# Sigmoid attention and an MLP on one core: the attention's matmuls put in order by four heads instead of by two

## The chip, the cores and the metric

The kernel runs on one NeuronCore of a Trainium2 chip. The metric is the device time of one execution in microseconds (us); lower is better. The kernel before takes 1061.03 us, the median of three timed runs (1060.72 to 1061.9).

## What is computed

```python
def _attn_ref(q, k, v) -> np.ndarray:          # (8 batches, 12 heads, 448, 64), float32
    S = q.shape[2]
    scale = 1.0 / np.sqrt(q.shape[-1])
    scores = scale * np.matmul(q, k.transpose(0, 1, 3, 2)) - np.log(S)
    attn = 1.0 / (1.0 + np.exp(-scores))
    return np.matmul(attn, v).astype(np.float32)

def _moe_ref(x, w_in, w_out) -> np.ndarray:    # x (3584, 768), w_in (768, 2048), w_out (2048, 768)
    h = x @ w_in
    g = h * (1.0 / (1.0 + np.exp(-1.702 * h)))
    return (g @ w_out).astype(np.float32)

# reference: x is the attention's output, (batch, position) by (head, 64); result = _moe_ref(x, w_in, w_out)
```

## The kernel before, in words

The program has two stages. In the first, attention runs for 48 pairs of heads (8 batches, 6 pairs each) while VectorE (DVE) and ScalarE (ACT) unpack the weights beside it. In the second, the MLP runs over seven blocks of 512 rows: one block directly (`first_block`, L794), the rest in two groups of three by a scheme with fewer products (`triple`). This change touches the first stage alone.

A pair n of heads brings q and k into `qkraw` (`load_pair`, L518); `split_pair` (L541) makes of it `qk`, a rounded part (a cast, ACT L442 or DVE L443) and the rest (DVE L448). The 448 positions are three chunks of 128 keys and 64 left over. TensorE (PE) then has four kinds of work:

- S, `scores` (L567, matmuls L577): per pair and chunk c six matmuls, 64 rows by 128 columns of the array, out of `qk`. Three chunks are one S of a pair, 18 matmuls.
- L, `scores_left` (L585, matmuls L593): the left-over keys of two pairs together, 64 rows by 64 columns, straight from `qkraw`; 4 matmuls that the trace shows as 8.
- V, `values` (L601, matmuls L608): the product of a chunk's sigmoids with v, 128 rows by 64 columns; 2 matmuls per chunk, shown as 4, so 12 for a pair.
- VL, `values_left` (L615, matmuls L621): the product of the left-over keys, 64 by 64, shown as 8.

Each of S's chunks and each L fills a tile `sc` of two PSUM banks and is read by one sigmoid on ACT (L563), which writes a tile `a` in SBUF. All V and VL of two pairs (four heads) add into one tile `av` of two banks; `to_x` (L638) copies it out on ACT (L645) or DVE (L646), and DMAs spill it to DRAM. The eight banks are four such places, `q0` to `q3`; `two_banks(place)` (L555) takes them in turn, so a tile must have been read before the fourth tile after it can be begun.

The order of the work is set before the program runs, by a planner (`Plan.run`): it knows tasks with estimated costs and dependencies, takes PE's units in the order of the list that `attention` returns, begins a unit when its tasks that are `alone` are ready, and gives ACT, DVE and the DMA queue (SP) the task with the earliest due time. What it writes is four fixed lists of instructions; on the chip each engine works through its own list in order and waits on semaphores. A task in `round_and_rest`, `to_x` and the like that may run on ACT or DVE is given to one of them by the planner.

In the list before, the units of two pairs (n even, then n odd) are: S of the even pair with V of the odd pair before it and that group's VL; L of both pairs; S of the odd pair with V of the even pair. V of a pair thus comes one unit after its S.

`BUFS` (L27) says how many buffers a tile has in turn: `qk` 2, `vraw` 3, `a` 7, `al` (the sigmoids of an L) 1, `x32` (the copy of `av`) 3.

Of the kernel before, what the change touches and what calls it, by code (L numbers as in the profile page):

```python
# [24 lines left out]
WARM = 26  # L25

BUFS = dict(  # L27
    qk=2, vraw=3, a=7, al=1, raw64=2, e=4, qkraw=5, x32=3,
    pair=2, wsplit=4, q0=1, q1=1, q2=1, q3=1, h0=1, h1=1,
)  # L30
SLOTS = dict(s=1536, g=2048, t=384)
# [48 lines left out]
class Plan:  # L80
# [15 lines left out]
    def task(self, engine, cost, emit, deps=(), uses=()):  # L96
        return self.either({engine: cost}, {engine: emit}, deps, uses)
# [227 lines left out]
def sigmoid_attention_mlp(ctx: ExitStack, tc: tile.TileContext, qk, v, w, out):  # L325
# [11 lines left out]
    NC = S // P  # L337
# [48 lines left out]
    plan = Plan()  # L386
# [166 lines left out]
    place_of = {}  # L553
# [13 lines left out]
    def scores(n, c, t_s, s, place):  # L567
        ps, a = two_banks(place), buffer("a")

        terms = ((0, 1), (1, 0), (0, 0)) if n else ((0, 0),)  # L570

        def emit():
            make(ps, ps.tag, [P, 2, 512], F32, f"sc{n}_{c}")
            src = [s.tile[:, 0], s.tile[:, 1]] if n else [s.tile]
            for i, (kk, qq) in enumerate(terms):
                for j, rows in enumerate(halves_of_rows):
                    nc.tensor.matmul(  # L577
                        ps.tile[:, j, :S], lhsT=src[kk][rows, S + c * P : S + (c + 1) * P], rhs=src[qq][rows, :S],
                        start=i == 0, stop=i == len(terms) - 1,
                    )  # L580

        t = task("PE", (0.7, 0.61, 0.61)[c] if n else 0.9, emit, t_s, [ps, s])
        return t, sigmoid(f"a{n}_{c}", a, ps, t), a

    def scores_left(n, sources, place):  # L585

        ps, a = two_banks(place), buffer("al")

        def emit():
            make(ps, ps.tag, [P, 2, 512], F32, f"sc{n}_{NC}")  # L590
            for cols, (_, src) in zip(halves_of_rows, sources):
                for j, rows in enumerate(halves_of_rows):
                    nc.tensor.matmul(  # L593
                        ps.tile[cols, j, :S], lhsT=src.tile[rows, S + NC * P :], rhs=src.tile[rows, :S],
                        start=True, stop=True, skip_group_check=True,
                    )

        t = task("PE", 0.8, emit, [t for ts, _ in sources for t in ts], [ps, *(b for _, b in sources)])
        return t, sigmoid(f"a{n}_{NC}", a, ps, t, "al"), a

    def values(n, c, t_a, a, t_v, vr, ps):  # L601

        def emit():
            if ps.tile is None:
                make(ps, ps.tag, [P, 2, 512], F32, f"av{n}")
            for j, cols in enumerate(halves_of_rows):
                at = ((n % 2 * 2 + j) * NC + c) * D
                nc.tensor.matmul(  # L608
                    ps.tile[cols, n % 2, :S], lhsT=vr.tile[:, at : at + D], rhs=a.tile[:, j],
                    start=c == 0, stop=False, skip_group_check=True,  # L610
                )

        return task("PE", (0.8, 0.75, 0.75)[c], emit, [t_a, t_v], [ps, a, vr])

    def values_left(t_a, a, t_v, vr, ps):  # L615

# [6 lines left out]
                        start=False, stop=True, skip_group_check=True,  # L623
                    )

        return task("PE", 0.95, emit, [t_a, t_v], [ps, a, vr])

    def places(b):

# [6 lines left out]
    copies = []  # L636
# [33 lines left out]
        ), x)  # L670


    firsts, urgent = [], []

    def attention():

        units, late, held_ = [], [], 0
        for n, (b, p) in enumerate(pairs):
            t_q, qkr, t_v, vr = load_pair(b, p)
            t_s, s = split_pair(b, p, t_q, qkr)
            firsts.append(t_s)
            left = scores_left(n, [first, (t_q, qkr)], held_ + 1) if n % 2 else None
            chunks = [scores(n, c, [t_s] if n else t_q[: c + 1], s, held_ + 1 + n % 2 + c) for c in range(NC)]
            run = [t for t, _, _ in chunks]  # L690
            if n % 2 == 0:
                first, chunks0, pair0 = (t_q, qkr), chunks, (b, p)
            else:

                units.append([left[0]])
                held_ += 1
                ps = two_banks(held_)
                both = [
                    [values(m, c, got[1], got[2], t_v, vr, ps) for c, got in enumerate(cs)]
                    for m, cs in ((n - 1, chunks0), (n, chunks))  # L700
                ]
                both[1].append(values_left(*left[1:], t_v, vr, ps))
                late.append(both[0])
                copied = len(copies)
                to_x(*pair0, both[1][-1], ps)
                urgent.append(copies[copied:])
            if n > 2 and n % 2:

                plan.early += [(t, run[0]) for t in urgent[n // 2 - 1]]

            with_v = late.pop(0) if late else []
            for t in run[2:] + with_v:
                t.alone = False
            units.append(run + with_v)
            if n % 2:
                late.append(both[1])
        units.append(late.pop())
        place_of["next"] = held_ + 1
        return units

    FULL, PIECE, XB, GB = slice(0, N2), NW_EL, NJ * T, 4 * T
# [563 lines left out]
```

## Time and profile before

| what | value |
|---|---|
| median of three timed runs | 1061.03 us |
| span of the profiled execution, first to last instruction | 1056.4 us |
| the median less the span | 4.6 us |
| PE matmul, busy | 1042.8 us, 99% of the span |
| DVE, ACT busy | 836.1 us (79%), 558.8 us (53%) |
| attention, from PE's first scores to the end of the last VL | 4.0 to 259.7 us |

The page gives the profiled execution no time of its own beside its span; the 4.6 us between the span and the median lie around it. Busy PE time comes from modelled ends of matmuls, so that places where one matmul waits for another inside PE count as busy too. How long a run of matmuls takes is therefore read from when the next run's work begins or ends: in the chain of waits, a piece reaches from the end of the piece before to its own end.

### The profile page before, as it was taken

How to read it: one execution, taken by the hardware profiler on the slowest of the kernel's cores; microseconds unless marked ns; L12 is line 12 of the kernel's file. 1: busy time of each engine (PE TensorE's matmuls, PEld its weight loads, DVE VectorE, ACT ScalarE, POOL GpSimd, SP SyncE). 2: the span in 40 equal slices, each digit the busy share in tenths (PEclk: the TensorE clock that was granted, in tenths of full speed). 3: DMA queues.
4: the chain of work that ended last, by engine and by line, in shares of the span. 5: the costliest groups of instructions: out<-in, count | busy, mean ns of one | idle time of the engine just before them, and what ended most of it. 6: DMA issues, size and time to landing. Idle time of an engine off the chain costs nothing.

```text
span 1056.4 us, 13606 instructions
## 1 busy us (share of the span) xinstructions
PE 1042.8 (99%) x5300; PEld 777.6 (74%) x5300; DVE 836.1 (79%) x734; ACT 558.8 (53%) x519; POOL 0.2 (0%) x4
## 2 busy tenths in 40 slices
PE   9999999999999999999999999999999999999997
PEld 5454545454788888888887788888888888788886
DVE  5978788772999856787998989999884596888684
ACT  7889888785664523434554444333443263434342
POOL 0000000000000000000000000000000000000000
PEclk9999999999999999999999999999999999999999
DMA  9999997883899997767656665959775545445765
GB/s 365 346 379 353 317 393 264 312 298 113 314 396 387 353 391 248 245 190 238 221 167 209 224 211 181 306 195 363 274 234 200 187 147 182 145 155 153 234 203 187
DMA packets 114704, 271.44 MB, mean 257 GB/s; under 512 B 10320, under 2 KB 80080, under 8 KB 112592
## 3 DMA queue, kind: packets, MB, share of 16 engines
q1 hardware_dynamic: 114640, 270.57, 73.6%
q8 instruction: 42, 0.69, 0.3%
q14 instruction: 22, 0.18, 0.0%
HBM read 185.60 MB, written 84.93 MB: 256 GB/s over the span
## 4 chain that ended last, share of the span: by engine, by line
PE 93%; DVE 2%; ACT 2%; DMA 1%; SPq 0%; issue 0%; ACTq 0%
PE p L782 57%; PE av L608 11%; PE sc L577 9%; PE h L782 6%; PE o_q L782 6%; PE av L621 2%; PE sc L593 2%; DMA c<-wc 1%; ACT a L563 1%; DVE gs L725 0%; ACT o L1138 0%; ACT xp L996 0%; DMA w<-c 0%; SPq L416 0%; DVE xp L1008 0%; DVE o L1139 0%
## 5 line engine op out<-in xcount | busy, mean ns | idle before, releaser
L782 PE MATMUL p<-gp,w 128*128 128x512 f32 x1440 | 329.1, 389 | 2.3 <-DVE gp L1008 0.9
L782 PE MATMUL p<-xp,w 128*128 128x512 f32 x1440 | 327.8, 389 | 1.0 <-DVE xp L1008 1.0
L782 PEld LDWEIGHTS p<-gp,w 128*128 128x128 f32 x1440 | 269.8, 188 | 60.4 <-DVE gp L1008 1.7
L782 PEld LDWEIGHTS p<-xp,w 128*128 128x128 f32 x1440 | 270.3, 188 | 57.4 <-DVE xp L1008 1.4
L563 ACT ACTIVATE a<-sc,bias 128x896 f32<-128x896 f32 x168 | 156.3, 1012 | 20.1 <-PE sc L577 12.0
L608 PE MATMUL av<-a,vraw 128*64 128x448 f32 x576 | 118.6, 547 | 0.0
L577 PEld LDWEIGHTS sc<-qk 64*128 64x128 f32 x846 | 75.9, 184 | 39.3 <-issue 17.1
L577 PE MATMUL sc<-qk 64*128 64x448 f32 x846 | 98.1, 373 | 1.5 <-DVE qk L448 1.5
L608 PEld LDWEIGHTS av<-a,vraw 128*64 128x64 f32 x576 | 37.1, 136 | 59.5 <-issue 59.0
L1008 DVE TENSOR_TENSOR gp<-h,gp 128x2048 fp32r<-128x2048 f32 x31 | 70.9, 2288 | 9.3 <-ACT gp L996 8.9
L1138 ACT COPY h<-p 128x2048 f32<-128x2048 f32 x18 | 33.7, 1874 | 82.5 <-PE p L782 53.1
L782 PE MATMUL o_q<-g,w 128*128 128x512 f32 x288 | 66.5, 389 | 1.2 <-ACT graw L838 1.2
L782 PE MATMUL h<-x,w 128*128 128x512 f32 x288 | 66.5, 389 | 1.0 <-ACT x L645 1.0
L996 ACT CAST gp<-h 128x2048 fp32r<-128x2048 f32 x23 | 44.0, 1912 | 44.0 <-PE p L782 36.7
L1172 DVE TENSOR_TENSOR h<-h,p 128x2048 f32<-128x2048 f32 x23 | 52.1, 2283 | 17.6 <-PE p L782 10.4
L782 PEld LDWEIGHTS h<-x,w 128*128 128x128 f32 x288 | 54.0, 188 | 13.0 <-ACT x L645 1.8
L782 PEld LDWEIGHTS o_q<-g,w 128*128 128x128 f32 x288 | 54.0, 188 | 12.8 <-ACT graw L838 1.6
L1138 ACT COPY o<-p 128x1536 f32<-128x1536 f32 x18 | 25.9, 1443 | 59.2 <-PE p L782 19.2
L448 DVE TENSOR_TENSOR qk<-qkraw,qk 128x896 fp32r<-128x896 f32 x47 | 51.2, 1090 | 6.5 <-ACT qk L442 5.7
L725 DVE TENSOR_TENSOR h<-h,h 128x2048 f32<-128x2048 f32 x24 | 54.7, 2284 | 0.1
L745 ACT CAST wc<-ws 128x384 fp32r<-128x384 f32 (+1 forms) x57 | 32.2, 580 | 41.0 <-DVE ws L725 26.0
L996 ACT CAST xp<-x 128x1536 fp32r<-128x1536 f32 x19 | 28.1, 1479 | 39.1 <-PE p L782 31.4
(108 smaller groups left out, 969.1 us busy)
## 6 DMA issues: line engine op xcount, KB each, us to landing
w<-c SPq DMA_DIRECT2D x140, 384.0 KB, 4.4
w<-c SPq DMA_DIRECT2D x52, 768.0 KB, 4.7
w<-w SPq DMA_DIRECT2D x16, 1536.0 KB, 10.5
c<-wc SPq DMA_DIRECT2D x56, 384.0 KB, 5.6
qkraw<-qk SPq DMA_DIRECT2D x47, 448.0 KB, 7.5
vraw<-v SPq DMA_DIRECT2D x24, 448.0 KB, 5.2
c<-wc SPq DMA_DIRECT2D x14, 768.0 KB, 6.9
c<-w SPq DMA_DIRECT2D x28, 384.0 KB, 3.8
```

The costliest lines, as they stand in the source:

```text
L448: lambda: nc.vector.tensor_tensor(lo(), src(), hi().bitcast(F32), op=ALU.subtract),
L563: nc.scalar.activation(a.tile, ps.tile[:, :, :S], AF.Sigmoid, bias=bias, scale=scale)
L577: nc.tensor.matmul(ps.tile[:, j, :S], lhsT=src[kk][rows, S + c * P : S + (c + 1) * P], rhs=src[qq][rows, :S], start=i == 0, stop=i == len( ...
L593: nc.tensor.matmul(ps.tile[cols, j, :S], lhsT=src.tile[rows, S + NC * P :], rhs=src.tile[rows, :S], start=True, stop=True, skip_group_chec ...
L608: nc.tensor.matmul(ps.tile[cols, n % 2, :S], lhsT=vr.tile[:, at : at + D], rhs=a.tile[:, j], start=c == 0, stop=False, skip_group_check=True,)
L725: return task("DVE", cost, lambda: nc.vector.tensor_tensor(out(), x(), y(), op=op), deps, uses)
L745: t_hi = on_either((act(n), lambda: nc.scalar.copy(into()[:, 0], node.view())), (cast(n), lambda: nc.vector.tensor_copy(into()[:, 0], node ...
L782: nc.tensor.matmul(ps, lhsT=ws[:, a, c * P : (c + 1) * P], rhs=x[:, d, k], start=start and i == 0 and j == 0, stop=stop and i == len(todo) ...
L996: t_hi = on_either((act(n), lambda: nc.scalar.copy(part(0)(), node.view())), (cast(n), lambda: nc.vector.tensor_copy(part(0)(), node.view())),
L1008: nc.vector.tensor_tensor(part(1)(), node.view(), part(0)().bitcast(F32), op=ALU.subtract)
L1138: t = on_either((act(self.n), lambda: nc.scalar.copy(view(), node.view())), (dve(self.n), lambda: nc.vector.tensor_copy(view(), node.view())),
L1172: nc.vector.tensor_tensor(view(), x.view(), y.view(), op=ALU.add if s0 == s else ALU.subtract)
```

## The change

The units of `attention` are now made per four heads (two pairs, a group g): one unit with all six chunks of S, one with all six V, then L of the next group, then this group's VL. The first unit has the first group's L at its end as well. All but the first task of a unit are no longer `alone`. Buffers move: `qk` 3, `vraw` 2, `a` 6, `al` 2, `x32` 2. PE's estimated costs in the planner are set anew; they are inputs of the planner and change no instruction by themselves.

```diff
--- before.py
+++ after.py
@@ -25,7 +25,7 @@
 WARM = 26
 
 BUFS = dict(
-    qk=2, vraw=3, a=7, al=1, raw64=2, e=4, qkraw=5, x32=3,
+    qk=3, vraw=2, a=6, al=2, raw64=2, e=4, qkraw=5, x32=2,
     pair=2, wsplit=4, q0=1, q1=1, q2=1, q3=1, h0=1, h1=1,
 )
 SLOTS = dict(s=1536, g=2048, t=384)
@@ -579,7 +579,7 @@
                         start=i == 0, stop=i == len(terms) - 1,
                     )
 
-        t = task("PE", (0.7, 0.61, 0.61)[c] if n else 0.9, emit, t_s, [ps, s])
+        t = task("PE", (0.8 if not c and n % 2 == 0 else 0.605) if n else (1.2, 1.4, 0.8)[c], emit, t_s, [ps, s])
         return t, sigmoid(f"a{n}_{c}", a, ps, t), a
 
     def scores_left(n, sources, place):
@@ -595,7 +595,7 @@
                         start=True, stop=True, skip_group_check=True,
                     )
 
-        t = task("PE", 0.8, emit, [t for ts, _ in sources for t in ts], [ps, *(b for _, b in sources)])
+        t = task("PE", 0.89, emit, [t for ts, _ in sources for t in ts], [ps, *(b for _, b in sources)])
         return t, sigmoid(f"a{n}_{NC}", a, ps, t, "al"), a
 
     def values(n, c, t_a, a, t_v, vr, ps):
@@ -610,7 +610,7 @@
                     start=c == 0, stop=False, skip_group_check=True,
                 )
 
-        return task("PE", (0.8, 0.75, 0.75)[c], emit, [t_a, t_v], [ps, a, vr])
+        return task("PE", 0.755 if c or n % 2 else 0.9, emit, [t_a, t_v], [ps, a, vr])
 
     def values_left(t_a, a, t_v, vr, ps):
 
@@ -623,7 +623,7 @@
                         start=False, stop=True, skip_group_check=True,
                     )
 
-        return task("PE", 0.95, emit, [t_a, t_v], [ps, a, vr])
+        return task("PE", 0.755, emit, [t_a, t_v], [ps, a, vr])
 
     def places(b):
 
@@ -670,7 +670,7 @@
         ), x)
 
 
-    firsts, urgent = [], []
+    firsts = []
 
     def attention():
 
@@ -680,42 +680,58 @@
 
 
 
-        units, late, held_ = [], [], 0
-        for n, (b, p) in enumerate(pairs):
-            t_q, qkr, t_v, vr = load_pair(b, p)
-            t_s, s = split_pair(b, p, t_q, qkr)
-            firsts.append(t_s)
-            left = scores_left(n, [first, (t_q, qkr)], held_ + 1) if n % 2 else None
-            chunks = [scores(n, c, [t_s] if n else t_q[: c + 1], s, held_ + 1 + n % 2 + c) for c in range(NC)]
+        units, place = [], 0
+
+        def take():
+            nonlocal place
+            place += 1
+            return place - 1
+
+        def four(g):
+
+            two = []
+            for n in (2 * g, 2 * g + 1):
+                b, p = pairs[n]
+                t_q, qkr, t_v, vr = load_pair(b, p)
+                t_s, s = split_pair(b, p, t_q, qkr)
+                firsts.append(t_s)
+                two.append((n, b, p, t_q, qkr, t_s, s))
+            return two, t_v, vr
+
+        def left_of(two):
+            return scores_left(two[1][0], [(t_q, qkr) for _, _, _, t_q, qkr, _, _ in two], take())
+
+        left = used = None
+        for g in range(len(pairs) // 2):
+            two, t_v, vr = four(g) if not g else ahead
+            chunks = [
+                scores(n, c, [t_s] if n else t_q[: c + 1], s, take())
+                for n, b, p, t_q, qkr, t_s, s in two for c in range(NC)
+            ]
             run = [t for t, _, _ in chunks]
-            if n % 2 == 0:
-                first, chunks0, pair0 = (t_q, qkr), chunks, (b, p)
-            else:
-
-                units.append([left[0]])
-                held_ += 1
-                ps = two_banks(held_)
-                both = [
-                    [values(m, c, got[1], got[2], t_v, vr, ps) for c, got in enumerate(cs)]
-                    for m, cs in ((n - 1, chunks0), (n, chunks))
-                ]
-                both[1].append(values_left(*left[1:], t_v, vr, ps))
-                late.append(both[0])
-                copied = len(copies)
-                to_x(*pair0, both[1][-1], ps)
-                urgent.append(copies[copied:])
-            if n > 2 and n % 2:
-
-                plan.early += [(t, run[0]) for t in urgent[n // 2 - 1]]
-
-            with_v = late.pop(0) if late else []
-            for t in run[2:] + with_v:
-                t.alone = False
-            units.append(run + with_v)
-            if n % 2:
-                late.append(both[1])
-        units.append(late.pop())
-        place_of["next"] = held_ + 1
+            if left is None:
+                left = left_of(two)
+                run.append(left[0])
+            units.append(run)
+            used = left
+            ps = two_banks(take())
+            out_ = [values(two[i // NC][0], i % NC, got[1], got[2], t_v, vr, ps) for i, got in enumerate(chunks)]
+            out_.append(values_left(*used[1:], t_v, vr, ps))
+            copied = len(copies)
+            to_x(*two[0][1:3], out_[-1], ps)
+            urgent = copies[copied:]
+            if g + 1 < len(pairs) // 2:
+                ahead = four(g + 1)
+                left = left_of(ahead[0])
+                out_.insert(-1, left[0])
+            units.append(out_)
+            if g:
+                plan.early += [(t, run[0]) for t in before_]
+                plan.early.append((left[1], run[0]))
+            before_, late = urgent, run
+            for u in (run, out_):
+                for t in u[1:]:
+                    t.alone = False
         return units
 
     FULL, PIECE, XB, GB = slice(0, N2), NW_EL, NJ * T, 4 * T
```

### What moves on PE

Two groups' border on PE before, around pairs 17 to 19. `scN_c` are the scores of pair N, chunk c (c = 3: an L), `avN` the products of pairs N and N+1; L577 is S, L608 V, L621 VL, L593 L.

```order
L577 MATMUL sc18_0_1167<-qk3_0_1096 128x448 x6
L577 MATMUL sc18_1_1176<-qk3_0_1096 128x448 x6
L577 MATMUL sc18_2_1185<-qk3_0_1096 128x448 x6
L608 MATMUL av16_1145<-a17_0_1135,vraw2_4_901 64x448 x2
L608 MATMUL av16_1145<-a17_1_1149,vraw2_4_901 64x448 x2
L608 MATMUL av16_1145<-a17_2_1157,vraw2_4_901 64x448 x2
L621 MATMUL av16_1145<-a17_3_1121,vraw2_4_901 64x448 x4
L593 MATMUL sc19_3_1212<-qkraw3_0_915 64x448 x2
L593 MATMUL sc19_3_1212<-qkraw3_1_1017 64x448 x2
L577 MATMUL sc19_0_1222<-qk3_1_1151 128x448 x6
L577 MATMUL sc19_1_1236<-qk3_1_1151 128x448 x6
L577 MATMUL sc19_2_1246<-qk3_1_1151 128x448 x6
```

S, V, VL, L and S again: three matmul shapes, of which every S and every V is a run for one pair. The same place now (line numbers below 670 are the same in both kernels):

```order
L577 MATMUL sc17_1_1132<-qk2_5_1032 128x448 x6
L577 MATMUL sc17_2_1142<-qk2_5_1032 128x448 x6
L608 MATMUL av16_1151<-a16_0_1107,vraw2_4_992 64x448 x2
L608 MATMUL av16_1151<-a16_1_1120,vraw2_4_992 64x448 x2
L608 MATMUL av16_1151<-a16_2_1140,vraw2_4_992 64x448 x2
L608 MATMUL av16_1151<-a17_0_1149,vraw2_4_992 64x448 x2
L608 MATMUL av16_1151<-a17_1_1156,vraw2_4_992 64x448 x2
L608 MATMUL av16_1151<-a17_2_1165,vraw2_4_992 64x448 x2
L593 MATMUL sc19_3_1179<-qkraw3_0_877 64x448 x2
L593 MATMUL sc19_3_1179<-qkraw3_1_981 64x448 x2
L621 MATMUL av16_1151<-a17_3_1083,vraw2_4_992 64x448 x4
L577 MATMUL sc18_0_1195<-qk3_0_1059 128x448 x6
```

The six V of a group stand in one run behind its six S, and L of the next group has moved ahead of VL.

### What moves on DVE

The list of DVE between the copies of two `av` tiles, before. L443 and L448 split a pair's q and k or a tile of x, L483 to L506 unpack a weight, L646 is the copy.

```order
L646 COPY x32_1_4_894<-av10_824 128x896
L499 TENSOR_TENSOR expo12_828<-expo12_828,sign12_852 128x1536
L506 SCALAR_TENSOR_TENSOR w32_12_835<-w32_12_835,expo12_828 128x1536
L443 CAST qk2_3_945<-qkraw2_3_800 128x896
L448 TENSOR_TENSOR qk2_3_945<-qkraw2_3_800,qk2_3_945 128x896
L483 TENSOR_SCALAR expo13_959<-w64_13_877 128x1536
L448 TENSOR_TENSOR x0_0_764<-x0_0_764 128x1536
L501 TENSOR_SCALAR w32_13_986<-w64_13_877 128x1536
L491 TENSOR_SCALAR expo13_959<-expo13_959 128x1536
L646 COPY x32_2_0_998<-av12_936 128x896
```

And now:

```order
L646 COPY x32_1_4_875<-av10_830 128x896
L506 SCALAR_TENSOR_TENSOR w32_12_788<-w32_12_788,expo12_753 128x1536
L443 CAST qk2_3_925<-qkraw2_3_759 128x896
L443 CAST x0_0_776<-x0_0_776 128x1536
L448 TENSOR_TENSOR qk2_3_925<-qkraw2_3_759,qk2_3_925 128x896
L448 TENSOR_TENSOR x0_0_776<-x0_0_776 128x1536
L483 TENSOR_SCALAR expo13_957<-w64_13_859 128x1536
L448 TENSOR_TENSOR qk2_4_953<-qkraw2_4_765,qk2_4_953 128x896
L501 TENSOR_SCALAR w32_13_969<-w64_13_859 128x1536
L491 TENSOR_SCALAR expo13_957<-expo13_957 128x1536
L646 COPY x32_2_0_990<-av12_938 128x896
```

Of the 24 copies 6 stood on DVE and 18 on ACT; now 20 stand on DVE and 4 on ACT, and the space between two of them on DVE is one group.

### What moves on ACT at the start

ACT's list from its first sigmoid, before; `aN_c` is the sigmoid of `scN_c`.

```order
L563 ACTIVATE a0_0_242<-sc0_0_236,bias_109 128x896
L563 ACTIVATE a0_1_251<-sc0_1_239,bias_109 128x896
L563 ACTIVATE a0_2_261<-sc0_2_248,bias_109 128x896
L563 ACTIVATE a1_3_272<-sc1_3_256,bias_109 128x896
L563 ACTIVATE a1_0_281<-sc1_0_263,bias_109 128x896
L563 ACTIVATE a1_1_293<-sc1_1_274,bias_109 128x896
L563 ACTIVATE a1_2_297<-sc1_2_283,bias_109 128x896
L442 CAST qk0_2_303<-qkraw0_2_232 128x896
L487 ACTIVATE sign8_308<-w64_8_230 128x1536
L442 CAST qk0_3_321<-qkraw0_3_234 128x896
```

And now:

```order
L442 CAST qk0_1_244<-qkraw0_1_226 128x896
L563 ACTIVATE a0_0_248<-sc0_0_236,bias_109 128x896
L563 ACTIVATE a0_1_254<-sc0_1_241,bias_109 128x896
L563 ACTIVATE a0_2_267<-sc0_2_250,bias_109 128x896
L563 ACTIVATE a1_0_284<-sc1_0_256,bias_109 128x896
L563 ACTIVATE a1_1_293<-sc1_1_269,bias_109 128x896
L563 ACTIVATE a1_2_299<-sc1_2_277,bias_109 128x896
L563 ACTIVATE a1_3_305<-sc1_3_286,bias_109 128x896
L487 ACTIVATE sign8_317<-w64_8_234 128x1536
L645 COPY x32_0_0_334<-av0_296 128x896
L563 ACTIVATE a3_3_356<-sc3_3_321,bias_109 128x896
L563 ACTIVATE a2_0_366<-sc2_0_339,bias_109 128x896
```

The cast of pair 1 stands first on ACT (it was on DVE), and in the second group the copy L645 stands ahead of the sigmoid of its L, `a3_3`. On the DMA queue the loads of pairs 2 and 3 (`qkraw`) now stand ahead of the first weight's load; before they stood behind it.

## Rows read from the trace of the kernel before

**Rows 1.** The page, sections 1 and 2: busy us; granted TensorE clock in tenths.

```profile
PE 1042.8 (99%) x5300; PEld 777.6 (74%) x5300; DVE 836.1 (79%) x734; ACT 558.8 (53%) x519; POOL 0.2 (0%) x4
...
PEclk9999999999999999999999999999999999999999
```

**Rows 2.** Chain that ended last, in order of time, attention's steady part: start, us, what.

```profile
20.15 0.75 PE sc L593 x8
20.90 2.02 PE sc L577 x18
22.92 2.41 PE av L608 x12
25.32 2.01 PE sc L577 x18
27.34 2.41 PE av L608 x12
29.74 0.91 PE av L621 x8
...
31.41 2.02 PE sc L577 x18
```

**Rows 3.** The same chain around the end of attention.

```profile
254.12 4.66 PE av L608 x24
258.78 0.96 PE av L621 x8
...
259.76 0.91 ACT x L645
...
260.71 16.63 PE h L782 x72
```

**Rows 4.** Timeline of PE, an S begun and whole: start, us, matmuls.

```profile
125.95 0.47 PE L577 MATMUL sc<-qk 64*128 64x448 f32 x2
...
125.95 2.09 PE L577 MATMUL sc<-qk 64*128 64x448 f32 x18
```

**Rows 5.** Timeline around the end of one VL: start, us, engine, line.

```profile
124.28 0.98 PE L621 MATMUL av<-a,vraw 64*64 64x448 f32 x8
125.33 0.91 ACT L645 COPY x<-av 128x896 f32<-128x896 f32 x1 [1.72 <-PE av L621]
126.17 3.70 ACT L563 ACTIVATE a<-sc,bias 128x896 f32<-128x896 f32 x4
```

**Rows 6.** The copies on DVE, and S's matmuls: ns min/median/max.

```profile
L646 DVE COPY x<-av x6: 1090/1091/1092, 30.7 to 230.4; 128x896 f32<-128x896 f32 x6
...
L577 PE MATMUL sc<-qk x36: 355/362/466, 125.9 to 132.1; 64*128 64x448 f32 x36
```

**Rows 7.** The chain at the start.

```profile
7.12 5.49 ACT a L563 x6
12.61 0.83 ACT qk L442
...
13.47 1.10 DVE qk L448
14.57 0.14 issue
14.71 2.12 PE sc L577 x18
```

**Rows 8.** Timeline at the start: pair 1's q and k arrive.

```profile
6.00 0.63 DVE L443 CAST qk<-qkraw 128x896 fp32r<-128x896 f32 x1 [5.00 <-DMA qkraw<-qk]
```

**Rows 9.** Stretch, length, busy PE, PEld, DVE, ACT; DMA share, GB/s; a wait.

```profile
62.17:114.71 52.54, 52.54 (x385) 26.38 (x380) 44.06 (x45) 48.00 (x49) 0.00 (x0) 1.00 0.96 357
...
DVE expo L483 <- DMA w<-w: 5.3, 2, 4.1
```

**Rows 10.** Timeline of DVE after attention: pieces of the second weight.

```profile
263.59 0.56 DVE L746 CAST w<-w 128x768 fp32r<-128x768 f32 x1 [18.18 <-DMA xd<-x]
264.25 1.83 DVE L748 TENSOR_TENSOR w<-w,w 128x768 fp32r<-128x768 f32 x2
```

## The prediction

> **What bounds the kernel now.** I read the page first: PE is busy 99% of the span at the full granted clock [rows 1]. So only fewer or cheaper PE microseconds, or one of PE's few gaps, can change the time. Next the chain of waits, in order of time. From 14.71 to 259.7 us it is PE alone, and it repeats every four heads: L .75, S 2.02, V 2.41, S 2.01, V 2.41, VL .91 [rows 2], in all 10.51 us. Matmuls of one kind do not take one time there. L and VL are the same eight 64 by 64 matmuls, but VL, behind V, takes .91, and L, behind VL, .75. At the end two V follow each other and take 4.66 [rows 3], so the second took 2.25 where each V behind an S takes 2.41. **A run thus pays about .16 for following matmuls of another shape.** For S I take the timeline: its first pair of matmuls ends .47 after the start and the ninth 2.09 [rows 4], so a pair costs 1.62 / 8 = .2025 and a whole S 1.82; in the chain it takes 2.01 or 2.02. S pays .19 to .20.
>
> The last reading is of the places where PE did wait: the start [rows 7] and the .95 between VL and the MLP [rows 3].
>
> **The steady part.** Before, four heads have five changes of shape: two into S (.39), two into V (.32), one into VL (.16); L follows VL without one. After: one into S (.20), one into V (.16), one from V into L (.16); VL follows L without one. No matmul is added. Saved: .87 - .52 = .35, so a group takes 10.16.
>
> What the order adds are waits inside a group, since only four places of two banks exist. I count from the end of VL, with the handoffs of the rows: a VL ending at 125.26 starts its copy at 125.33, .07 later [rows 5]; an end on DVE starts PE .14 later [rows 7]; sigmoids follow each other by (3.70 - 1.01) / 3 = .90, with 1.01 for the last [rows 5].
> - The third chunk takes the place of `av`. Chunks end at .20 + .61 each, so its first matmul would end at 1.62 and, being .36 long [rows 6], start at 1.26. The copy is now mostly on DVE, 1.09 [rows 6]: .07 + 1.09 + .14 = 1.30. **.04 late.** On ACT (.91) it would be in time.
> - The fifth and sixth chunk wait for the first two sigmoids. The first chunk ends at .81, its sigmoid runs from .88 to 1.89, PE may go on at 2.03; needed at 2.47. The second ends at 2.79, so 2.93; needed at 3.08. Nothing, with .15 to spare.
> - The products take the third chunk's place: its sigmoid ends at 3.69, so 3.83; needed at about 3.78. The .04 above covers most of it.
>
> I take .08 per group; below I bound it by 0, above by .35, the point where the group saves nothing. The other new waits cover themselves: L's sigmoid has until the fourth chunk of the next S, PE's waits for its own older matmuls were met a group ago, and `vraw` with two buffers is loaded a whole group before its V.
>
> Here a rule is weighed. Rows: the sigmoids of six chunks last 6 x .90 = 5.4 us and the matmuls 3.84, and four places take up the difference, as just worked out. The Trainium skill, page TensorEngine Tiling (Array Packing), section PSUM Bottleneck, says that tiling speeds TensorE but not the emptying of PSUM, which may become the bound. If it did from the first chunk, each group would lose 1.5 us, and 22 groups 33. No row here shows that; its milder form is a rival.
>
> **DVE** is what the copies are moved to. It is busy 44.06 of 52.54 us [rows 9], five groups, so 8.8 per group. Fourteen more copies in 24 groups add .64: 9.45 of 10.16. That leaves .7 of a group. Where DVE waits for a weight (twice, 5.3 us in all, in 157 us of before [rows 9]), the copy behind it is late and PE with it. I put .5 us in all on this; between 0 and 8.
>
> **The start.** Before, PE stood 1.5 us until 14.71: pair 2's cast came on ACT behind six sigmoids, then DVE's rest, 1.10, and .14 [rows 7]. After, pair 1's cast comes first on ACT: q and k are there at 6.00 [rows 8], + .83 + 1.10 + .14 [rows 7] = 8.1, call it 8.2. Then PE runs S 2.02, L .91, both V 4.66, the next L .91 and VL .75: 17.45. Pair 2 is ready long before, since its load has moved ahead of a weight's. In the second group the list puts the copy ahead of L's sigmoid on ACT, so the first sigmoid of S starts .9 late; fifth and sixth chunk and the products then wait some .5, .3 and .2. So the third group's S starts at 17.45 + 10.16 + 1.0 = 28.6. Before, S of pair 5 starts at 31.41 [rows 2] with S of pair 4 (2.01) done as well: 29.4 for the same work. **Gain .8.**
>
> **The end.** From there 21 groups and a last one without L remain: 21 x 10.16 + 3.84 + 4.66 + .91 = 222.8, against 259.7 - 29.4 = 230.3. **Gain 7.5**, less 22 x .08 = 1.7 and the .5 for DVE. The gap behind attention (from 259.76, the start of the copy, to 260.71 [rows 3]) exists since `h0_0` needs `q0`, where `av` lay. By the same counting of places `av` of the last group now lies in `q3` (place 191), and in the order the first matmul of the MLP waits for PE alone. **Gain .95.** Next in line there is the second weight: DVE had its pieces between 263.6 and 266.1 [rows 10], PE takes them half of 16.63 after 260.71 [rows 3], at 269.0; with PE .95 earlier 2 us are left. The wait of about 1.1 that follows, for the activation before the first `o0` products, stays. The rest of the program has the same PE list, so it only shifts.
>
> **Sum:** .8 + 7.5 - 1.7 - .5 + .95 = 7.05. The sum is made against a span of 1056.4, so 1049.4; the runs' median lies 4.6 above the span, and I predict **1054.0**. A measurement here can tell about .2%, 2.1 us, from no change.
>
> **Rivals.**
> - *Stalls eat the gain.* DVE's list is nearly full and the copy is the one instruction that PE waits for. If copies come on average .35 late instead of .04, 22 groups give back 6.8: 1060.8. For it speaks how little of a group DVE has left; against it, that .7 of a group is left on average, so that lateness need not add up from group to group. Decides from .3 per group.
> - *The cost is not in the change of shape,* but comes back elsewhere in a joined run (say at each new `qk`). Then only start and gap are won, .8 + .95, and the stalls lost, 1.7: 1061.0. Against it stands the 4.66 [rows 3]. That it does what it says to the order is seen in the rows of PE.
> - *Slower: the sigmoids pace S.* ACT works in order, and now in 18 of 24 groups a cast, sign or exponent step, each waiting for a load or DVE, stands between the sixth sigmoid and that of L. If this puts the first sigmoid of S .9 late in every group, as it is in the second, each group loses 1.0 in place of .08, 22 groups 20: 1074. It starts to cost from .15 late and turns the sign from about .45. Against it: ACT has 7 x .90 of sigmoids in 10.16, so some 3.8 us for one or two other steps, and before it waited for a weight once. The page named above is of this kind; that the rows show four places covering the run is why its chance is small.
>
> **Chances.** Forecast .80 (1050.8 with no stall and no late copy, to about 1057.5); stalls .10; cost elsewhere .03; slower .07. Faster by over .2% (under 1058.9): .80 and a third of the stalls, .83; within: .10; slower .07. The range leaves out the rivals' far ends: 1051.0 to 1058.5.
>
> **What would show it.** In the profile after: pieces of about 3.8 (S x36), 4.66 (V x24), .91 (L) and .75 (VL) in the chain; 10.2 to 10.3 from group to group; the MLP's first matmul at about 253.2 instead of 260.71, straight behind VL. A late copy would show as PE idle before `sc` with DVE L646 as releaser, pacing sigmoids as PE idle before `sc` or `av` with ACT L563. The forecast is wrong if groups take 10.4 or more, or if a new gap stands in the MLP: DVE had 18 us of rest before 263.59 [rows 10], of which the copies take part, and if a weight is late there, the gain is given back.

## The result, and the profile after

The changed kernel takes 1051.3 us, the median of four executions (1050.97 to 1051.68), against 1060.88 for the kernel before beside it (four, 1060.4 to 1061.9): a ratio of 0.9911, 95% interval 0.9898 to 0.9924. That is faster, if by under 1%, and 1051.3 lies in the predicted range, near its lower end and 2.7 us under the predicted time. The gain is 9.6 us where the sum had 7.05. Between the two profiled executions the span went from 1056.4 to 1049.3, and that is 7.1. So the sum met the two profiles and missed 2.5 us of the times; where these are is the main question of the experiments.

The page, sections 1 and 2 (answers to [rows 1]):

```profile
PE 1037.9 (99%) x5300; PEld 779.4 (74%) x5300; DVE 852.8 (81%) x755; ACT 542.2 (52%) x498; POOL 0.2 (0%) x4
...
PEclk9999999999999999999999999999999999999999
```

PE is still the bound at the full granted clock, with the same 5300 matmuls in 4.9 us less. DVE has 16.7 us more, ACT 16.6 less.

The chain of waits, in order of time, from the first scores (answers to [rows 2, 3, 7]); columns are start, us, what:

```profile
4.06 5.94 PE sc L577 x30
10.00 0.91 PE sc L593 x8
10.91 4.66 PE av L608 x24
15.57 0.91 PE sc L593 x8
16.48 0.75 PE av L621 x8
17.24 2.83 PE sc L577 x24
...
20.97 0.87 PE sc L577 x6
...
21.87 4.73 PE av L608 x24
...
28.26 3.92 PE sc L577 x36
32.18 4.66 PE av L608 x24
36.84 0.91 PE sc L593 x8
37.76 0.75 PE av L621 x8
38.51 3.91 PE sc L577 x36
...
252.39 0.91 PE av L621 x8
253.30 8.84 PE h L798 x38
```

A group is now S 3.91, V 4.66, L .91, VL .75. From 28.26 to 38.51 it takes 10.25 (before 10.51, predicted 10.24 with its wait). The second group's S, from 17.24, takes 4.63 and its V 4.73. The MLP follows the last VL directly at 253.30; before it came 1.0 after it, at 260.71.

The timeline of one group (busy stretches; in brackets the idle time before them and what ended it):

```profile
79.47 3.98 PE L577 MATMUL sc<-qk 64*128 64x448 f32 x36
79.60 1.09 DVE L646 COPY x<-av 128x896 f32<-128x896 f32 x1 [0.23 <-PE av L621]
80.44 3.71 ACT L563 ACTIVATE a<-sc,bias 128x896 f32<-128x896 f32 x4 [0.56 <-PE sc L577]
80.75 2.32 PEld L577 LDWEIGHTS sc<-qk 64*128 64x128 f32 x24 [0.17 <-DVE x L646]
```

This is the one wait left inside a group: the third chunk's weights (13th of S's 36 loads) are loaded .06 after the copy's end, where the sum had .14 and a wait of .04. S pays .07 for it, 3.91 in place of the 3.84 counted without waits. S takes 3.91 to 4.00 in the 22 groups from 28.26 on. DVE, which now holds most copies, had less to spare in its fullest groups than the .7 us a group of the prediction: in the five groups from 58.98 on it was busy 49.67 of 51.26 us, so .3 a group were left, and S still took 3.91 to 3.96 there (columns as in [rows 9], answers to it):

```profile
58.98:110.24 51.26, 51.26 (x380) 26.73 (x380) 49.67 (x51) 42.91 (x44) 0.00 (x0) 1.00 1.01 383
```

In the second group ACT has the copy ahead of L's sigmoid, the first of seven here:

```profile
17.30 0.91 ACT L645 COPY x<-av 128x896 f32<-128x896 f32 x1 [1.76 <-PE av L621]
18.11 6.41 ACT L563 ACTIVATE a<-sc,bias 128x896 f32<-128x896 f32 x7
```

### The profile page after: what moved, and what is told of

It is laid out like the page before. It is cut to its first block, busy times and chain, and to the rows that moved or that the text cites. A ratio compares the mean times of both kernels' runs of the same rounds, so it can differ in the third digit from the quotient of the medians.

```text
span 1049.3 us, 13577 instructions
## 1 busy us (share of the span) xinstructions
PE 1037.9 (99%) x5300; PEld 779.4 (74%) x5300; DVE 852.8 (81%) x755; ACT 542.2 (52%) x498; POOL 0.2 (0%) x4
## 4 chain that ended last, share of the span: by engine, by line
PE 93%; DVE 3%; ACT 2%; DMA 1%; issue 0%; ACTq 0%
PE p L798 57%; PE av L608 11%; PE sc L577 9%; PE h L798 6%; PE o_q L798 6%; PE sc L593 2%; PE av L621 2%; DMA out<-o 1%; DVE gp L1024 1%; DVE h L741 1%; DVE gs L741 0%; ACT gp L1012 0%; DMA c<-w 0%; DVE xp L1024 0%; DVE o L1155 0%; DVE o L1188 0%
## 5 line engine op out<-in xcount | busy, mean ns | idle before, releaser
L608 PE MATMUL av<-a,vraw 128*64 128x448 f32 x576 | 113.5, 543 | 0.0
L577 PEld LDWEIGHTS sc<-qk 64*128 64x128 f32 x846 | 75.5, 184 | 27.2 <-PE sc L593 16.2
L577 PE MATMUL sc<-qk 64*128 64x448 f32 x846 | 94.8, 373 | 0.0
L608 PEld LDWEIGHTS av<-a,vraw 128*64 128x64 f32 x576 | 39.2, 137 | 63.7 <-issue 45.3
L448 DVE TENSOR_TENSOR qk<-qkraw,qk 128x896 fp32r<-128x896 f32 x47 | 50.7, 1088 | 6.6 <-ACT qk L442 6.0
L1024 DVE TENSOR_TENSOR xp<-x,xp 128x1536 fp32r<-128x1536 f32 x22 | 38.6, 1753 | 13.9 <-ACT xp L1012 13.8
```

What stands on the lines that cost most here:

```text
L448: lambda: nc.vector.tensor_tensor(lo(), src(), hi().bitcast(F32), op=ALU.subtract),
L577: nc.tensor.matmul(ps.tile[:, j, :S], lhsT=src[kk][rows, S + c * P : S + (c + 1) * P], rhs=src[qq][rows, :S], start=i == 0, stop=i == len( ...
L608: nc.tensor.matmul(ps.tile[cols, n % 2, :S], lhsT=vr.tile[:, at : at + D], rhs=a.tile[:, j], start=c == 0, stop=False, skip_group_check=True,)
L1024: nc.vector.tensor_tensor(part(1)(), node.view(), part(0)().bitcast(F32), op=ALU.subtract)
```

## The experiments

Each is timed over several executions, with the kernel before on the same chip beside it. All edits are to the changed kernel if not said otherwise.

**1. The kernel before once more.** No edit.

> The kernel before once more, unchanged, with the span of every execution beside its time. The prediction put the time 4.6 us above the span, from 1061.03 and a span of 1056.4; the four executions of the changed kernel lie 1.8 us above their spans. Reading A: what lies around the span is a property of the program, 4.6 us here in every execution, and the change took 2.8 us off it. Reading B: it is 1.8 us for both kernels, the spans of the timed executions of before are 1058.6 to 1060.1, and the profiled execution was 2 to 3 us shorter than the timed ones. Under B the change is worth some 9.6 us inside the span of timed executions, and the sum of 7.05 was made against a span that the timed executions do not have.

1059.94 us (11 executions, 1059.09 to 1061.38); beside it 21 of the same program, 1058.1 to 1061.78, median 1060.71. The profiled execution took 1060.92 with a span of 1059.1: 1.8 lies around it, as in the four of the changed kernel. **Reading B holds.** The 4.6 us of the prediction, which the text ahead of it puts around the span, were 1.8 around it and 2.8 by which the profiled execution was shorter than the median. The chain of this execution (left out: the split of pair 2, and the groups between):

```profile
3.06 10.09 DMA qkraw<-qk
...
33.59 2.02 PE sc L577 x18
...
262.84 16.64 PE h L782 x72
```

and ACT and PE at the start, in the timeline:

```profile
13.17 0.94 ACT L442 CAST qk<-qkraw 128x896 fp32r<-128x896 f32 x1 [1.20 <-DMA qkraw<-qk]
...
15.38 3.62 PE L577 MATMUL sc<-qk 64*128 64x448 f32 x18 [2.61 <-DVE qk L448]
```

In the profile shown ahead of the prediction, pair 2's cast went straight on behind six sigmoids at 12.61 [rows 7]; its load had come in time. Here it is waited for 1.2 us, S of pair 2 begins at 15.38 in place of 14.71 and takes 3.62 in place of 2.12, and everything behind it is 2.1 to 2.2 late (33.59 against 31.41, 262.84 against 260.71). The later load is .67 of this; the other 1.50, the longer S, stand in TensorE's granted clock, which the page's slices of 26 us are too coarse to show. By stretch, columns as in [rows 9] (the clock, as a share of the full one, is third from the end):

```profile
14.00:16.00 2.00, 0.62 (x4) 0.64 (x6) 1.86 (x2) 2.00 (x3) 0.00 (x0) 0.83 1.08 444
16.00:18.00 2.00, 2.00 (x14) 1.93 (x12) 2.00 (x4) 1.46 (x2) 0.00 (x0) 0.50 1.03 436
18.00:20.00 2.00, 2.00 (x12) 0.96 (x12) 2.00 (x2) 1.91 (x2) 0.00 (x0) 0.81 0.93 374
```

From about 15.3 to 18.8 (the .83 and .81 place the ends) the clock was .50, the lower of its two levels (1.2 in place of 2.4 GHz). Just before, PE had stood idle for 2.61 us; in the profile ahead of the prediction it stood idle for 1.53 there and the clock stayed at 1.00. So a late load cost here its own .67 and then 1.50 in clock; that the gap brought the fall is read from their order and was not tested, and the gap's length alone does not decide it: in the first kernel of experiment 7 PE stood idle for 2.5 us ahead of S of pair 1, and the clock stayed at 1.00. The start of before thus cost 2.2 us more in this execution than in that one. How often the clock falls is not shown, since only these two executions have a trace, but the mean clocks of the timed ones point to about half: of the 55 executions of this kernel in the experiments, 28 have a mean of .996 or .997, as this one, and took 1060.44 to 1062.36 (median 1061.04); the other 27, at .998 to 1.000, took 1058.10 to 1061.38 (median 1059.32). A mean does not tell where the clock was lost, and in experiment 8 executions with .997 are not the longer ones.

**2. Loads of pairs 2 and 3 ahead of the first weight, in the kernel before.** The weight is 1536 KB, a pair's q and k 448 KB.

```diff
             firsts.append(t_s)
+            if n in (2, 3):
+                plan.early += [(t, units[2][-1]) for t in t_q]
```

> The kernel before, with the loads of q and k of pairs 2 and 3 ahead of the first weight's load on the DMA queue, as the changed kernel has them; the order of TensorE's work stays the old one. In the profiled execution of before S of pair 2 began at 14.71 after a gap of 1.5 and took 2.1; in the second one it began at 15.38 after gaps of 2.9 and took 3.6, and the span was 2.7 longer. Theory: the load behind the weight lands at another time in each execution, and this start is what makes the executions of before differ by 3 us; with the load ahead of the weight S of pair 2 begins at about 13.2 without a gap. Median 1056.8 (1.5 below the shortest of before, 1058.1), executions within 1 us of each other. Rival: the 2 to 3 us lie elsewhere (in the MLP's DMA waits); then the median is 1059 to 1060.7, and the spread stays at 2 to 3 us.

1056.55 us (1055.62 to 1057.73), ratio 0.9961 (0.9948 to 0.9973): 4.2 less than before's 1060.78 beside it, with TensorE's order of attention untouched. The spread stayed at 2.1, wider than expected. The chain:

```profile
12.56 2.02 PE sc L577 x18
...
29.16 2.02 PE sc L577 x18
```

S of pair 2 begins at 12.56 without a gap, S of pair 5 at 29.16, and the granted clock is 1.00 throughout the start. So part of what the change brings could be had by the load alone. (The planner also gave pair 2's and 3's casts to DVE here; that is in the 4.2.) Why the spread stayed was not followed.

**3. That load late, in the changed kernel.** The first weight is loaded ahead of pairs 2 and 3, as before the change.

```diff
-        plan.early.append((load, firsts[min(2 + pair, len(firsts) - 1)]))
+        plan.early.append((load, firsts[min(2 + pair, len(firsts) - 1)] if decoded else lefts[1]))
```

(`lefts` holds the L tasks.) Beside it ran the changed kernel without an edit, and the kernel of experiment 9, all on one chip.

> The changed kernel once more, unchanged, as the mark for the two runs beside it: 1051.3, executions between 1050.9 and 1051.7 as before. If executions differ by 1 us or more, differences of that size between single profiles prove nothing.

> The changed kernel with the first weight's load ahead of the loads of pairs 2 and 3 on the DMA queue, as in the kernel before; the order of TensorE's work stays the new one. Theory: in the new order S of pair 2 begins at 17.2 in place of 13 to 15, and the loads of both pairs land at 12.5 to 14.3, so the order hides them; what is left is a cast that stands ahead of L's sigmoid in the second group, where a copy stood: median within 1 us of the changed kernel, 1051.5. Rival: the late loads cost here what they cost in the old order, 3 to 4 us, and the executions spread by 2 to 3 us: 1054.5 to 1055.5.

The changed kernel took 1052.37 there (1051.91 to 1053.23), 1.1 more than in its first four executions, and gained 8.6 on before (1060.93, ratio 0.9926); so differences of 1 us between separate measurements prove nothing. With the load late it took 1051.68 (1051.62 to 1052.42). **The new order doesn't care where the load stands**: S of pair 2 isn't due before 17, and the third group's S began at 28.18 (28.88 beside it), the MLP at 254.01 (253.81). The same loss has two remedies, an earlier load or a later use; the change applies both, and they don't add.

The chain of the unedited kernel beside it, whose execution took 1052.14:

```profile
28.88 3.95 PE sc L577 x35
...
253.81 16.56 PE h L798 x72
```

**4. Two more changes of shape.** All copies on DVE here, and L amid the six V.

```diff
-                out_.insert(-1, left[0])
+                out_.insert(3, left[0])
```

> All copies on DVE, as in the run beside it, and L of the next group in the middle of the six products (V V V L V V V VL): the same matmuls, with two more changes of shape in each of 23 groups. Theory (a run pays .16 for following another shape): a group takes 10.24 + .32 = 10.56, the chain shows 2.41, .91, 2.41, .91 and 3.91, and the time is 23 x .32 = 7.4 us longer than with all copies on DVE alone, 1057.9 if that is 1050.5. Rival (what the change saved lies elsewhere, in waits or in the start of each run on new data): no difference beyond 1 us.

1058.91 us (1058.31 to 1059.56), 7.7 above the 1051.24 of experiment 6. One group in the chain:

```profile
39.93 3.91 PE sc L577 x36
43.84 2.41 PE av L608 x12
46.25 0.91 PE sc L593 x8
47.16 2.41 PE av L608 x12
49.57 0.91 PE av L621 x8
50.48 3.91 PE sc L577 x36
```

10.55 against 10.25: the same matmuls, .30 more for two changes. The two V take 4.82 in place of 4.66, VL .91 in place of .75. The price of .16 that the prediction read from before is confirmed by adding it. From the fourth group's S to the MLP it is 260.77 - 39.93 = 220.84 against 215.11 in experiment 6, so .29 for each of 20 groups. The 7.7 is not all of this kind: about 1.1 of it lies ahead of the fourth group, where S of pair 1 began .4 later and a copy of the third group came late on DVE.

**5. The places moved by one.**

```diff
-        units, place = [], 0
+        units, place = [], 1
```

> The changed kernel with every place counted one further, so that the last av lies in q0 again, which the first tile of the MLP needs. Theory: the gap between the last VL and the MLP returns, .95 to 1.03 us with the copy on ACT as releaser; the MLP begins at about 254.3 in place of 253.3. If nothing later takes it up, the end comes 1.0 later: span 1050.3, median 1052.3. Rival: a later wait of the MLP (ACT's graw, 1.17, or the weight's pieces on DVE) takes it up, and span and median stay within .3 of the changed kernel's 1049.3 and 1051.3.

1052.65 us (1051.38 to 1052.85), 1.4 above experiment 6, measured beside it. The timeline behind the last VL:

```profile
254.36 0.91 ACT L645 COPY x<-av 128x896 f32<-128x896 f32 x1 [3.20 <-PE av L621]
...
255.32 3.04 PE L798 MATMUL h<-x,w 128*128 128x512 f32 x12 [1.02 <-ACT x L645]
```

The gap is back with its 1.02 and its releaser. That the end came later by just this can't be told from these times, since this execution also began S of pair 1 later (8.66 against 7.91).

**6. All copies on DVE.** In `to_x`:

```diff
-        c = on_either((0.97, lambda: nc.scalar.copy(xb.tile, ps.tile[:, :, :S])),
-                      (1.09, lambda: nc.vector.tensor_copy(xb.tile, ps.tile[:, :, :S])), [t], [xb, ps], rows)
+        def copy():
+            rows()
+            nc.vector.tensor_copy(xb.tile, ps.tile[:, :, :S])
+
+        c = task("DVE", 1.09, copy, [t], [xb, ps])
```

> The changed kernel with all 24 copies of av on DVE (it has 4 on ACT). Theory: in the second group the copy no longer stands ahead of L's sigmoid on ACT, so S there takes 3.9 us in place of 4.6 (the pieces 2.83, .87, .87 with .07 between them), and attention ends .7 to .8 earlier; the third chunk still waits some .06 in each group for the copy (S x36 3.91 in the chain). Median 1050.5. Rival: the four copies were on ACT because DVE was behind there; then DVE is late in these groups, PE idles before sc with the copy as releaser, and the time is the same or up to 2 us longer (1051.3 to 1053).

1051.24 us (1051.18 to 1051.55): no gain. Half of the expectation holds: the second group took 10.24. One group showed what the rival said, a copy that came late:

```profile
161.52 1.07 DVE L647 COPY x<-av 128x896 f32<-128x896 f32 x1
...
162.65 1.08 PE L577 MATMUL sc<-qk 64*128 64x448 f32 x8 [0.17 <-DVE x L647]
```

The MLP began at 253.03, .27 earlier than after the change, and the end was no earlier; where in the MLP the rest went was not followed.

**7. The sigmoids made late.** In the first kernel the copy is a task of ACT, with the same edit as above. The second has all copies on DVE, and VL ahead of L:

```diff
-                out_.insert(-1, left[0])
+                out_.append(left[0])
```

> The changed kernel with all 24 copies of av on ACT (it has 4 there), where the list puts them between L's sigmoid and the first sigmoid of S. Theory (the rival of the prediction in which the sigmoids pace S, at a known dose): L's sigmoid ends .33 after VL, the copy .91 later, so the third chunk waits .12 in place of .06, the first sigmoid of S comes .36 late, the sixth chunk waits some .1 and the products .2. A group takes .35 longer, 22 groups 7.7, median 1059.0 (range 1056 to 1061). Rival: four places cover this delay too; the third chunk's wait is all, and the median is within 1.5 us of 1051.2.

> All copies on DVE, and VL of the group ahead of L of the next one in place of behind it; the number of changes of shape is the same. The copy then begins .75 earlier, and L's sigmoid .75 later. Theory: the third chunk's wait (.06 per group) goes, but the first sigmoid of S begins 1.08 after S in place of .88, so the sixth chunk waits .05 and the products some .2: a group takes 10.4, the time is 3 to 4 us longer than with L first (1051.24), 1054.5. Rival: four places cover the .2 as well; then only the third chunk's wait goes, and the time is 1050.0.

All on ACT: 1055.3 us (1054.88 to 1056.97). Most of its 4 us lie outside the groups: in the profiled execution S of pair 1 began 1.2 later (9.10), and PE waited 1.9 and 1.1 in the MLP where the changed kernel waited .9 and nothing. A group takes 10.31, .07 more and not .35:

```profile
101.58 3.99 PE L577 MATMUL sc<-qk 64*128 64x448 f32 x36
101.90 0.90 ACT L647 COPY x<-av 128x896 f32<-128x896 f32 x1
102.68 5.52 ACT L563 ACTIVATE a<-sc,bias 128x896 f32<-128x896 f32 x6
...
105.56 4.73 PE L608 MATMUL av<-a,vraw 128*64 128x448 f32 x24
```

The first sigmoid begins 1.03 after the end of VL (101.65), .15 later than the .88 it could, not .36: twice the next instruction of ACT began .1 before the one ahead was over (copy to sigmoid .78 for a copy of .90). V then begins .07 after the third sigmoid, 2.88 behind the start of the first.

VL first: 1052.16 us (1050.89 to 1052.81), not to be told from 1051.24, and not the 1054.5 expected. A group takes 10.25 (S 3.84 to 3.90, V mostly 4.73): the copy's wait goes and the sigmoids' comes, nothing is won. In one group of it ACT was truly late; a cast of x that waited for a load stood ahead of L's sigmoid:

```profile
68.37 1.47 ACT L442 CAST x<-x 128x1536 fp32r<-128x1536 f32 x1 [0.92 <-DMA x<-xd]
...
69.75 4.59 ACT L563 ACTIVATE a<-sc,bias 128x896 f32<-128x896 f32 x5
...
73.50 0.60 PE L608 MATMUL av<-a,vraw 128*64 128x448 f32 x2
```

S's first sigmoid begins .90 after L's, 1.65 after S began at 69.00: .77 late. **Three doses are thus measured,** against 3.84 for S and 4.66 for V without a wait: .15 late costs .15 (3.92 and 4.73; a part of it is the third chunk's wait for the copy, which ended at 102.80), .77 costs .73 (4.50 and 4.73), and .89 in the second group of the changed kernel (18.11 + .90 - 17.24 - .88) costs .86. Since V can begin 2.88 after the first sigmoid, a delay costs from .08 on, where the prediction had .15, and then nearly its whole length.

**8. The new order with the old buffers.**

```diff
-    qk=3, vraw=2, a=6, al=2, raw64=2, e=4, qkraw=5, x32=2,
+    qk=2, vraw=3, a=7, al=1, raw64=2, e=4, qkraw=5, x32=3,
```

> The new order with the old numbers of buffers (qk 2, vraw 3, a 7, al 1, x32 3). Theory: with one al buffer the sigmoid of the next L waits for VL of this group, so it begins .07 after VL and the first sigmoid of S 1.08 after it in place of .88: the products wait some .2, and the time is 3 to 5 us longer than the changed kernel's, 1055; two qk buffers are no limit, since a pair's split has 6 us between two runs of S. Rival A: the buffers give nothing, 1051.3. Rival B: two qk are the limit, PE idle before sc with DVE's rest L448 as releaser, 1060 or more.

1058.05 us (1057.13 to 1059.76), 6 to 7 above the changed kernel. It was none of the causes expected: the groups without trouble take 10.29, .04 more, but in three groups a copy came late on DVE, 3.5 us in all, in the last group the copy stood on ACT ahead of the sigmoids and S took 4.64, and the waits in the MLP were longer. The largest:

```profile
81.20 1.08 DVE L646 COPY x<-av 128x896 f32<-128x896 f32 x1
...
82.33 0.88 PE L577 MATMUL sc<-qk 64*128 64x448 f32 x6 [1.63 <-DVE x L646]
```

S had begun at 79.22. The chain leads from this copy back to a reload of x from DRAM, whose cast and rest stood ahead of it on DVE. This is the prediction's first rival, realised by a list that the planner makes from other buffer numbers. Which of the five numbers does it was not tried.

**9. L right behind the first pair, a version for both weak places of the start.** Pair 0's three chunks, then L, then pair 1's.

```diff
-            run = [t for t, _, _ in chunks]
-            if left is None:
-                left = left_of(two)
-                run.append(left[0])
+            chunks, run = [], []
+            for n, b, p, t_q, qkr, t_s, s in two:
+                for c in range(NC):
+                    chunks.append(scores(n, c, [t_s] if n else t_q[: c + 1], s, take()))
+                    run.append(chunks[-1][0])
+                if left is None:
+                    left = left_of(two)
+                    run.append(left[0])
```

> The changed kernel with L of the first group right behind the three chunks of pair 0 in place of behind those of pair 1. What moves with it: pair 1's cast goes to DVE, the first copy goes behind or off L's sigmoid on ACT, 22 copies stand on DVE. Theory: the gap of up to 1.5 before S of pair 1 is filled by L (.9), and the second group's S takes 3.9 in place of 4.6: the third group's S begins at 26.6 in place of 28.26, the MLP at 251.7 in place of 253.3, and if the MLP keeps the lead, the median is 1049.6, 1.6 below the changed kernel's. Rival: DVE's list, which holds nearly all copies then, is late in some groups, or a wait of the MLP for a store or a weight takes the lead back, as with all copies on DVE: 1051.0 to 1051.5.

1050.84 us (1049.88 to 1052.08), 1.5 below the changed kernel beside it (1052.37), with five executions each that overlap a little. The third group's S begins at 27.66 and the MLP at 252.60, 1.2 earlier than beside it (26.6 and 251.7 were expected), although pair 1's load landed .66 later (its 5.40 against 4.74):

```profile
1.65 5.40 DMA qkraw<-qk
...
8.97 2.09 PE sc L577 x18
...
17.39 3.95 PE sc L577 x36
...
27.66 3.91 PE sc L577 x36
```

It is the fastest version tried; that it beats the changed kernel rests on this one comparison.

## Why the prediction was right, and where not

- **The mechanism held.** A change of shape costs .16 to .20: read from before, seen after (S, V, L and VL take 3.84 plus a wait, 4.66, .91, .75 as forecast), and shown by experiment 4. The Trainium skill, page TensorEngine Tiling (Array Packing), section Key Properties, says that changing the tiling mode drains TensorE. No row shows the drain itself; a price at each change of shape, and none from L to VL, which share one, agrees with it.
- **The steady part:** predicted 7.5 - 1.7 - .5 = 5.3 from the third group to the MLP without the gap. In the two profiles: 259.69 - 29.4 = 230.3 before (260.71 less the 1.02 gap), 253.30 - 28.26 = 225.0 after, so 5.25. The waits of .07 to .16 in 22 groups came to 2.2, which is 1.7 and DVE's .5 together; a late DVE as such was not seen after the change, but in experiments 3, 4, 6 and 8.
- **The gap:** .95 predicted; 1.02 went, and came back with the places in experiment 5.
- **The start, the term that was mis-sized.** ".8" compared with the one execution in the profile; there it was 1.1 (29.4 less 28.26), because the second group lost .86 and not 1.0, and began .2 earlier. Between experiment 1's execution, which is about as long as the median of before, and the unedited one of experiment 3 it is 33.59 - 2.02 - 28.88 = 2.7: before lost 2.2 more there, .7 by the load and 1.5 by the clock that fell behind it, and the changed kernel lost .6 more by pair 1's load. The prediction had named the moved load and called pair 2 "ready long before", and gave it no worth, since in that profile the load was not what S waited for; a fall of the clock it did not think of.
- **The 4.6.** "The runs' median lies 4.6 above the span" took an execution that was 2.8 shorter than the median for a typical one. With 1.8 the same sum gives 1051.2 for the changed kernel, whose executions vary less (by .7 and 1.3 in the two measurements). That is why the time was 2.7 high and the gain 2.5 short at once. The lower end of the range, 1050.8, was meant for no waits at all (1.7, .5 and the second group's 1.0 left out); the waits came, 2.2 and .86, and the time lies near that end by this offset alone.
- **The MLP** gave back .3: in the first two profiles a wait of .86 for a store (ACT L899) is new and one of .6 for a load is gone. In experiment 1's and the unedited one of experiment 3 it gave back .3 too, with both waits at 1.0, so what else took it is open. The prediction looked for such a gap at the second weight only. It is partly luck, then, that the sum of 7.05 met the 7.1 of the profiles: the start was .3 short and the MLP .3 over.
- **The rivals.** Late copies and late sigmoids both exist, in experiments 6 to 8. A first sigmoid .9 late in every group was priced at 1.0, and .89 late cost .86; but the changed kernel's lists make it late in one group alone. The 1.5 per group that the prediction worked out for sigmoids that bound S from the first chunk did not come: four places cover a run of six sigmoids that begins in time.

Put together for two executions near the medians (1060.92 and 1052.14): start 2.7, steady 5.3, gap 1.0, MLP -.3 make 8.7 between these two profiles (spans 1059.1 and 1050.4). In the old order the load alone brought more than the 2.7 of the start, 4.2 (experiment 2).

## What to carry to other kernels

Where matmuls of several tile shapes alternate, read a run's price from the chain by what stood before it, and put runs of one shape together as far as the buffers in PSUM cover the engines that empty them. A profile is one execution: ask which of its waits hang on a transfer's landing time, since the next execution may land later, and lost clock can come on top (1.50 us behind an idle time of 2.61, in experiment 1): where a run takes longer than the same run elsewhere, read the granted clock of that stretch. Compare the profiled execution's own time with the median before a span is turned into a time. When a change of order also moves a load, try the load alone.

## What was not expected of the hardware

The third transfer of the program, q and k of pair 1, took between 4.31 and 5.40 us from issue to landing in the chains shown or read here, and S of pair 1 moved with it (8.09 after 4.31 in experiment 6, 8.52 after 4.74 in the unedited kernel). The load of pair 2 behind a 1536 KB weight took 10.09 in one execution, and with the weight behind it (experiment 2) its cast began at 9.41, as the row below shows. The Trainium skill, page DMA: Bandwidth & Descriptors, section Queues, rings and completion order, says that each DMA engine consumes descriptors in ring order; the 10.09 and the 9.41 agree with it.

```profile
9.41 0.63 DVE L443 CAST qk<-qkraw 128x896 fp32r<-128x896 f32 x1 [1.60 <-DMA qkraw<-qk]
```

The other surprise is the clock: in one execution of the kernel before (experiment 1) it fell to .50 for some 3.4 us behind an idle time of PE, and S of pair 2 took 1.50 us longer there without a wait.
